# Another bank for the y of the second chunk, and a fixed order between the copies of the state and the low part

## The chip, the cores and the metric

The kernel runs on one core of a Trainium2 chip. The metric is device time in microseconds (us) of one execution, as a median over several. The profile comes from one more execution, taken by the hardware profiler; its span is the time from its first to its last instruction.

## What is computed

The inputs are `x` (4 x 8 x 768 x 32), a decay `a`, `B` and `C` (4 x 8 x 768 x 16), and two weight matrices. A linear recurrence over the 768 positions of each of 4 sequences and 8 heads is computed in chunks, with a state of 16 x 32 per head that goes from one chunk to the next. Its output, 3072 tokens of 256 numbers, goes through a two-layer network:

```python
for c in range(nc):
    M = einsum('bhin,bhjn->bhij', Cc, Bc) * L          # L: causal decay inside the chunk
    y[:, :, sl] = einsum('bhij,bhjd->bhid', M, xc) + einsum('bhin,bhnd->bhid', Cc, state) * decay_to_i
    state = decay_full * state + sum_j(Bc * xc * decay_from_j)
h = x @ w_in                 # 3072 x 256 times 256 x 2048
return (h - tanh(h)) @ w_out # 2048 x 256
```

The result does not depend on the length of a chunk; the kernel takes its own.

## The kernel before

**The recurrence.** A chunk has 112 positions (`Q = P - N`), the last of a sequence fewer; 7 chunks make a sequence, 28 the whole (`ck` = 0 to 27). A chunk's work is a chain: products of C and B into the tile `att` on TensorE (lines 377 in the first three chunks, 437 and 443 later), exponentials on ScalarE (384, 447), their product on VectorE (389, 451), the causal mask on GpSimd (394, 454) which leaves `lt`, and then `chunk_y` (472 to 529). `chunk_y` does the following.

- Line 488: TensorE makes the output y of the chunk from `lt` and `x`. The first 16 rows of `x` of a chunk hold the state that enters it.
- Line 496: TensorE makes the next state from the weighted B (`bw`, made by GpSimd on line 330 for two chunks at a time) and the same `x`, into other columns of the same tile y.
- Line 501: ScalarE copies the state into the first 16 rows of the next chunk's `x`, in four copies.
- Line 508: ScalarE copies y into `xh`, rounded to the format in which TensorE is fast (the high part).
- Line 513: VectorE makes `xl`, y minus the high part (the low part).

The tile y has one buffer, one bank of PSUM (`ps_y`, tag "y"). So line 488 of a chunk waits until lines 501, 508 and 513 of the chunk before are done. ScalarE and VectorE are also kept from reading the one bank at the same time: an instruction of one of them on it waits for the other's instructions that stand before it in the written order. Another single bank, `ps_o` (tag "po"), takes sums of the decays at the start (`pq2`, read by line 786) and from then on the output of the second layer.

**The network.** `mm1(t, u)` (line 547, 12 matmuls of 128 x 256) makes one 256 x 256 piece of h for tile t of 256 tokens from `xh`, `xl` and the split weights `wh`, `wl`; `act` takes tanh on ScalarE (561), h - tanh(h) on VectorE (565), a high part on ScalarE (569) and a low part on VectorE (576); `mm2` (line 597, 12 matmuls) adds it to the output tile `o`. The first tile needs chunks 0, 1 and 2. The first four tiles are taken together in sweeps over pairs of u (u = 0 and 1 first), so that the weights, which `conv` (282 to 306) splits mostly on VectorE, are made as they come.

**The order of the instructions** is made before the kernel runs. Each piece of work is an `op(engine, cost, function, r=, w=, dma=, after=)` of the class `Order` (46 to 188), which records what it must wait for. `schedule` is a list scheduler with the estimated costs, and `issue` takes the best of 16 jittered rounds from a fixed seed (133908) and writes the instructions in the order of their planned starts. The order of each engine is then fixed; in the run, each engine waits for what its next instruction needs. The instructions of `chunk_y` are three to six such ops: TensorE's work of one chunk, four copies of the state, the high part, the low part. The chunks from `JOINT` on have the products of the next chunk in the same TensorE op.

**DMAs** are issued by the SyncE queue (SP). The decays' partial sums go to DRAM and come back in eight transfers for chunks 3 to 9 and eight for the later chunks (`get_parts`, lines 772 and 774); chunk 3's products on line 437 need the first eight.

Of the kernel before, what the change touches and what calls it, by code (L numbers as in the profile page):

```python
# [10 lines left out]
F32 = mybir.dt.float32  # L11
# [9 lines left out]
P = 128  # L21
NB, H, S, D, N = 4, 8, 768, 32, 16
# [10 lines left out]
CPG = 2  # L33
# [14 lines left out]
class Order:  # L48
# [12 lines left out]
    def slot(self, tag, bufs):  # L61
        k = self.count[tag] = self.count.get(tag, -1) + 1
        self.fresh[f"{tag}#{k}"] = tag, f"{tag}#{k - bufs}"
        return f"{tag}#{k}"
# [8 lines left out]
    def __call__(self, eng, cost, fn, r=(), w=(), dma=0, after=()):  # L73
        i = len(self.ops)
        hard = {self.writer[n] for n in r if n in self.writer} | set(after)
        soft, chain = set(), set()
        for n in w:
            hard |= self.readers.pop(n, set())
            if n in self.writer:
                j = self.writer[n]  # L80
                if dma and self.ops[j][0] == "DMA":
                    chain.add(j)
                    hard |= self.before[n]
                else:
                    hard.add(j)
            self.writer[n] = i
            whole = self.whole.get(n, n)
            if whole in self.fresh:
                tag, old = self.fresh.pop(whole)
                for o in (old, *self.parts.get(old, ())):  # L90
                    self.dead.add(o)
                    hard |= self.readers.pop(o, set())
                    if o in self.writer:
                        hard.add(self.writer[o])
                if tag in self.taken:
                    soft.add(self.taken[tag])
                self.taken[tag] = self.made[whole] = i
            elif whole in self.made:
                soft.add(self.made[whole])
        for n in (*r, *w):  # L100
            assert n not in self.dead and n not in self.fresh and n in self.writer, n
        for n in r:
            self.readers.setdefault(n, set()).add(i)
        deps = {j: self.lag(self.ops[j][0], eng) if j in hard else 0.0 for j in (hard | soft) - {i}}
        self.ops.append((eng, cost, fn, deps))
        if dma:

            self.ops.append(("DMA", max(0.25, dma / self.RATE), None, {i: 1.4, **{j: 0.0 for j in chain}}))
            for n in r:
                self.readers[n].add(i + 1)  # L110
            for n in w:
                self.writer[n], self.before[n] = i + 1, hard - {i}
        return i
# [77 lines left out]
def tile_ssm_moe(ctx: ExitStack, tc: tile.TileContext, a, x, bn, bc, wts, out):  # L191
# [7 lines left out]
    ps_o = ctx.enter_context(tc.tile_pool(name="ps_o", bufs=1, space=PSUM))  # L199
    ps_a = ctx.enter_context(tc.tile_pool(name="ps_a", bufs=1, space=PSUM))  # L200
    ps_y = ctx.enter_context(tc.tile_pool(name="ps_y", bufs=1, space=PSUM))

    op = Order()
    slot = op.slot
    grp = {g: {} for g in range(NG)}
    chs = {c: {} for c in range(NCK)}
    raws, gs, po, n_po, obs, misc = {}, {}, {}, {}, {}, {}

    chunks, ends = {}, 0
    for t in range(NT):  # L210
        b, j = divmod(t, S // TT)
# [130 lines left out]
    def qlen(ck):  # L342
        return QL if ck % CPB == CPB - 1 else Q
# [80 lines left out]
    def chunk_a(ck):  # L424

        d, k, q = grp[ck // CPG], chs[ck], qlen(ck)
        n_l = k["n_l"] = [slot("lt", NL)]
        n_a = k["n_a"] = slot("att", 1)  # L430

        def fn_p():
            at_ = ps_a.tile([P, 4, 4 * P], F32, tag="att", name=f"att{ck}")
            at_ = k["a"] = at_[:, :, 0 : 4 * q].rearrange("p i (k q) -> p i k q", k=4)
            for i in range(4):
                r = slice(32 * i, 32 * i + 9)
                nc.tensor.matmul(out=at_[:, i, 0:2, :], lhsT=lt_c[r, ck], rhs=rt_c[r, :, ck, N : N + q],  # L437
                                 start=True, stop=True)
            bb, cc = operands(ck)
            for w in range(2):  # L440
                for i in range(4):
                    r = slice(32 * i, 32 * i + N)
                    nc.tensor.matmul(out=at_[:, i, 2 + w, :], lhsT=bb[r, w], rhs=cc[r, w, 0:q], start=True, stop=True)  # L443

        def fn_e():
            k["l"] = p3.tile([P, H, Q], F32, tag="lt", name=f"lt{ck}", bufs=NL)
            nc.scalar.activation(k["l"][:, :, 0:q].rearrange("p (i w) q -> p i w q", i=4), k["a"][:, :, 0:2, :], AF.Exp)  # L447

        def fn_m():
            lt = k["l"][:, :, 0:q].rearrange("p (i w) q -> p i w q", i=4)  # L450
            nc.vector.tensor_tensor(out=lt, in0=k["a"][:, :, 2:4, :], in1=lt, op=ALU.mult)  # L451

        def fn_s():
            nc.gpsimd.affine_select(out=k["l"][:, :, 0:q], in_=k["l"][:, :, 0:q], pattern=[[0, H], [1, q]],  # L454
                                    compare_op=ALU.is_ge, fill=0.0, base=N, channel_multiplier=-1)

        s = ck >= SPAN[0].stop
        k["rest"] = fn_e, fn_m, fn_s
        k["pe_a"] = fn_p, [d["n_bc"], l_c[s], r_c[s]], [n_a]
        if ck < JOINT:  # L460
            op("PE", 0.65, fn_p, r=k["pe_a"][1], w=k["pe_a"][2])
            chunk_b(ck)
# [9 lines left out]
    def chunk_y(ck):  # L472

        d, k, q = grp[ck // CPG], chs[ck], qlen(ck)
        b, c = divmod(ck, CPB)
        cg = ck % CPG
        n_y = slot("y", 1)
        last = c == CPB - 1
        if c == 0:
            seq[b]["n_xh"] = op.pieces(slot("xh", 2), CPB)  # L480
            seq[b]["n_xl"] = op.pieces(slot("xl", 2), CPB)
        n_xh, n_xl = seq[b]["n_xh"][c], seq[b]["n_xl"][c]

        def fn():
            y = k["y"] = ps_y.tile([P, 2 * H * D], F32, tag="y", name=f"y{ck}")
            for hg in range(2):
                for h in range(4):
                    nc.tensor.matmul(out=y[D * h : D * h + D, hg * Q : hg * Q + q],  # L488
                                     lhsT=d["x"][:, cg, P * hg + D * h : P * hg + D * h + D],
                                     rhs=k["l"][:, 4 * hg + h, 0:q], start=True, stop=True)  # L490
            if not last:

                for w in range(2):
                    for i in range(4):
                        h = 2 * i + w
                        nc.tensor.matmul(out=y[D * i : D * i + N, H * D + D * w : H * D + D * w + D],  # L496
                                         lhsT=d["b"][:, cg, N * h : N * h + N], rhs=d["x"][:, cg, D * h : D * h + D],
                                         start=True, stop=True)

        def fn_c(i):  # L500
            nc.scalar.copy(grp[(ck + 1) // CPG]["x"][0:N, (ck + 1) % CPG, 2 * D * i : 2 * D * i + 2 * D],  # L501
                           k["y"][D * i : D * i + N, H * D : H * D + 2 * D])

        def fn_h():
            if c == 0:
                seq[b]["xh"] = p3.tile([P, 2, S], F32R, tag="xh", name=f"xh{b}", bufs=2)
            k["yv"] = k["y"][:, 0 : 2 * Q].rearrange("p (g q) -> p g q", g=2)[:, :, 0:q]
            nc.scalar.copy(seq[b]["xh"][:, :, c * Q : c * Q + q], k["yv"])

        def fn_l():  # L510
            if c == 0:
                seq[b]["xl"] = p3.tile([P, 2, S], F32R, tag="xl", name=f"xl{b}", bufs=2)
            nc.vector.tensor_tensor(out=seq[b]["xl"][:, :, c * Q : c * Q + q], in0=k["yv"],  # L513
                                    in1=seq[b]["xh"][:, :, c * Q : c * Q + q].bitcast(F32), op=ALU.subtract)

        r, w, cost = [*k["n_l"], d["p_x"][cg], d["n_bw"]], [n_y], 0.5 if last else 0.7
        if JOINT <= ck + 1 < NCK:

            chunk_a(ck + 1)
            fn_p, r_a, w_a = chs[ck + 1]["pe_a"]  # L520
            op("PE", cost + 0.45, lambda: (fn(), fn_p()), r=r + r_a, w=w + w_a)
            chunk_b(ck + 1)
        else:
            op("PE", cost, fn, r=r, w=w)
        if not last:
            for i in range(4):
                op("ACT", 0.2, lambda i=i: fn_c(i), r=[n_y], w=[grp[(ck + 1) // CPG]["p_x"][(ck + 1) % CPG]])
        op("ACT", 0.36, fn_h, r=[n_y], w=[n_xh])
        op("DVE", 0.4, fn_l, r=[n_y, n_xh], w=[n_xl])


    def mm1(t, u):
# [116 lines left out]
    after = cp.tile([P, P], F32, name="after")  # L649
# [119 lines left out]
    def get_parts(i, k, sl):  # L769
# [17 lines left out]
       r=[n_pq2], w=["wdec"])  # L787
# [95 lines left out]
```

## Time and profile before

| | |
|---|---|
| Median of 3 runs | 349.26 us (344.88 to 349.93) |
| The profiled execution | 344.03 us, span 342.3 us |
| TensorE busy | 328.4 us, 96% of the span |
| VectorE busy | 227.5 us, 66% |
| ScalarE busy | 192.8 us, 56% |
| GpSimd busy | 52.1 us, 15% |
| Granted TensorE clock, mean | 0.979 |

How to read it: PE is TensorE, PEld its weight loads, DVE VectorE, ACT ScalarE, POOL GpSimd, SP SyncE. The table of windows gives the busy time of each engine in a stretch of the span, with the number of instructions, then the granted TensorE clock (PEclk, 1.00 is full speed), the busy share of the DMA engines and what they moved. A row of the timeline gives start and duration in us, engine, line, operation, tiles and how many instructions were merged in it (neighbours overlap, since instructions are pipelined); in square brackets is the idle time of the engine just before it, with the instruction that is taken to have ended it. A row of the waits gives total time, number and longest.

### The profile page before, as it was taken

The numbers are of one execution on the slowest core, as the hardware profiler recorded it, in microseconds if no ns is written. First come the engines' busy times: TensorE is split into PE (matmuls) and PEld (weight loads), VectorE is DVE, ScalarE is ACT, GpSimd is POOL, SyncE is SP. The second block draws the span as 40 slices with busy tenths as digits, with TensorE's granted clock in tenths as the row PEclk, the third lists the DMA queues.
The fourth block names the chain that finished last, engine by engine and source line by source line (L and its number), as shares of the span: only waits on it lengthen the run. The fifth ranks groups of instructions, "written<-read, shape, count | busy, mean of one in ns | idle before, by whom it ended". The sixth has DMA issues, their size and how long they took to land.

```text
span 342.3 us, 8855 instructions
## 1 busy us (share of the span) xinstructions
PE 328.4 (96%) x3756; PEld 317.9 (93%) x3756; DVE 227.5 (66%) x339; ACT 192.8 (56%) x403; POOL 52.1 (15%) x69
## 2 busy tenths in 40 slices
PE   8669879999999999999999999999999999999995
PEld 7658769999999999999999999999999999999995
DVE  5998999988889656744755644644655654644552
ACT  8866698767453445634745644634645654634441
POOL 1535443101000001210211210210211110100000
PEclk9956999999999999999999999999999999999999
DMA  5939595800000022300301210210100000100000
GB/s 173 280 92 288 138 314 129 250 23 21 11 2 0 2 64 77 104 1 2 97 9 31 65 29 2 63 29 2 63 3 3 31 2 2 33 0 2 33 0 32
DMA packets 12471, 21.39 MB, mean 62 GB/s; under 512 B 2848, under 2 KB 7648, under 8 KB 12432
## 3 DMA queue, kind: packets, MB, share of 16 engines
q1 hardware_dynamic: 12432, 20.84, 20.9%
q8 instruction: 29, 0.48, 0.6%
q14 instruction: 10, 0.08, 0.1%
HBM read 17.51 MB, written 3.32 MB: 61 GB/s over the span
## 4 chain that ended last, share of the span: by engine, by line
PE 88%; DMA 3%; DVE 3%; SPq 2%; ACT 1%; issue 1%; POOL 1%; POOLq 0%
PE ph L547 40%; PE o L597 40%; PE y L488 4%; PE att L443 3%; DMA raw<-w_d 2%; DMA bc<-bc_d 1%; PE att L437 1%; SPq L232 1%; PE y L496 1%; DVE lt L451 1%; DVE wm L295 0%; DVE gl L576 0%; DVE wv L299 0%; POOL bw L330 0%; ACT x L501 0%
## 5 line engine op out<-in xcount | busy, mean ns | idle before, releaser
L561 ACT ACTIVATE g<-ph 128x512 f32<-128x512 f32 x96 | 57.4, 598 | 82.5 <-PE ph L547 78.7
L565 DVE TENSOR_TENSOR g<-ph,g 128x512 f32<-128x512 f32 x96 | 66.1, 689 | 55.0 <-ACT g L561 54.1
L547 PE MATMUL ph<-xh,wh 128*128 128x256 f32 x384 | 101.5, 287 | 0.0
L547 PE MATMUL ph<-xh,wl 128*128 128x256 f32 x384 | 100.3, 282 | 0.0
L576 DVE TENSOR_TENSOR gl<-g,gh 128x512 fp32r<-128x512 f32 x96 | 68.4, 713 | 28.7 <-ACT gh L569 27.4
L569 ACT CAST gh<-g 128x512 fp32r<-128x512 f32 x96 | 59.3, 619 | 34.1 <-DVE g L565 32.9
L547 PE MATMUL ph<-xl,wh 128*128 128x256 f32 x384 | 77.1, 282 | 0.0
L547 PEld LDWEIGHTS ph<-xh,wh 128*128 128x128 f32 x384 | 73.2, 191 | 1.4 <-issue 0.4
L547 PEld LDWEIGHTS ph<-xh,wl 128*128 128x128 f32 x384 | 73.2, 191 | 0.0
L597 PE MATMUL o<-gh,wh 128*128 128x256 f32 x384 | 62.3, 284 | 0.0
L597 PE MATMUL o<-gh,wl 128*128 128x256 f32 x384 | 60.7, 280 | 0.0
L597 PE MATMUL o<-gl,wh 128*128 128x256 f32 x384 | 60.7, 280 | 0.0
L547 PEld LDWEIGHTS ph<-xl,wh 128*128 128x128 f32 x384 | 59.6, 191 | 0.0
L597 PEld LDWEIGHTS o<-gh,wh 128*128 128x128 f32 x384 | 51.9, 188 | 1.5
L597 PEld LDWEIGHTS o<-gl,wh 128*128 128x128 f32 x384 | 52.0, 188 | 0.0
L454 POOL TENSOR_SCALAR_AFFINE_SELECT lt<-lt 128x896 f32<-128x896 f32 (+1 forms) x25 | 28.3, 1131 | 155.4 <-DVE lt L451 152.8
L597 PEld LDWEIGHTS o<-gh,wl 128*128 128x128 f32 x384 | 51.9, 188 | 0.0
L451 DVE TENSOR_TENSOR lt<-att,lt 128x896 f32<-128x896 f32 (+1 forms) x25 | 26.7, 1067 | 11.0 <-ACT lt L447 10.9
L447 ACT ACTIVATE lt<-att 128x896 f32<-128x896 f32 (+1 forms) x25 | 22.6, 905 | 11.0 <-PE att L443 10.6
L501 ACT COPY x<-y 16x64 f32<-16x64 f32 x96 | 19.4, 202 | 7.9 <-DVE xl L513 6.9
L488 PE MATMUL y<-lt,x 128*32 128x112 f32 (+1 forms) x448 | 17.1, 272 | 6.5 <-POOL bc L337 2.5
L330 POOL TENSOR_TENSOR bw<-braw,wdec 128x256 f32<-128x256 f32 x14 | 12.5, 896 | 52.8 <-PE y L496 47.1
(70 smaller groups left out, 227.2 us busy)
## 6 DMA issues: line engine op xcount, KB each, us to landing
raw<-w_d SPq DMA_DIRECT2D x16, 512.0 KB
x<-x_d SPq DMA_DIRECT2D x14, 256.0 KB
bc<-bc_d SPq DMA_DIRECT2D x56, 60.0 KB
out_d<-ob SPq DMA_DIRECT2D x24, 128.0 KB
braw<-bn_d SPq DMA_DIRECT2D x14, 112.0 KB
cum<-parts SPq DMA_DIRECT2D x1, 168.0 KB
lt_c<-cum SPq DMA_DIRECT2D x4, 27.0 KB
rt_c<-cum SPq DMA_DIRECT2D x4, 27.0 KB
```

What stands on the lines that cost most here:

```text
L330: nc.gpsimd.tensor_tensor(out=d["b"].rearrange("p c (h n) -> p c h n", h=H), in0=d["braw"].rearrange("p c (h n) -> p c h n", h=H), in1=wd. ...
L447: nc.scalar.activation(k["l"][:, :, 0:q].rearrange("p (i w) q -> p i w q", i=4), k["a"][:, :, 0:2, :], AF.Exp)
L451: nc.vector.tensor_tensor(out=lt, in0=k["a"][:, :, 2:4, :], in1=lt, op=ALU.mult)
L454: nc.gpsimd.affine_select(out=k["l"][:, :, 0:q], in_=k["l"][:, :, 0:q], pattern=[[0, H], [1, q]], compare_op=ALU.is_ge, fill=0.0, base=N, ...
L488: nc.tensor.matmul(out=y[D * h : D * h + D, hg * Q : hg * Q + q], lhsT=d["x"][:, cg, P * hg + D * h : P * hg + D * h + D], rhs=k["l"][:, 4 ...
L501: nc.scalar.copy(grp[(ck + 1) // CPG]["x"][0:N, (ck + 1) % CPG, 2 * D * i : 2 * D * i + 2 * D], k["y"][D * i : D * i + N, H * D : H * D + ...
L547: nc.tensor.matmul(out=ph[:, j, :], lhsT=w_[:, u, 0, k, j * P : (j + 1) * P], rhs=d[("xh", "xl")[p]][:, k, ts], start=p == 0 and k == 0 an ...
L561: nc.scalar.activation(g, gs[t, u][0], AF.Tanh)
L565: nc.vector.tensor_tensor(out=g, in0=ph, in1=g, op=ALU.subtract)
L569: nc.scalar.copy(gh, gs[t, u][1])
L576: on.tensor_tensor(out=gl, in0=g, in1=gh.bitcast(F32), op=ALU.subtract)
L597: nc.tensor.matmul(out=po[t, seg][:, e, :], lhsT=w_[:, u, 1, j, e * P : (e + 1) * P], rhs=g[:, j, :], start=u == seg[0] and k == 0 and j = ...
```

## The change

Three things are changed.

- The y of chunk 1 is made in the bank of the output (`ps_o`, tag "po") instead of `ps_y`. All other chunks keep `ps_y`.
- After line 508, which now stands first, the order of the copies of the state and the low part is fixed. For chunks 0 and 1 the low part comes after the four copies. For all later chunks that have a next state, the four copies come after the low part. Before, the planner chose.
- In `Order`, a transfer into a tile into which an earlier transfer goes gets a soft edge from the op that issued the earlier one (`j - 1`), so the planner issues them in the order in which they are written. It adds no wait.

```diff
@@ class Order, __call__ @@
                 if dma and self.ops[j][0] == "DMA":
                     chain.add(j)
+                    soft.add(j - 1)
                     hard |= self.before[n]
@@ chunk_y @@
-        n_y = slot("y", 1)
+
+        n_y = slot("po" if ck == 1 else "y", 1)
...
-            y = k["y"] = ps_y.tile([P, 2 * H * D], F32, tag="y", name=f"y{ck}")
+            y = k["y"] = (ps_o if ck == 1 else ps_y).tile([P, 2 * H * D], F32, tag="po" if ck == 1 else "y", name=f"y{ck}")
...
-        if not last:
-            for i in range(4):
-                op("ACT", 0.2, lambda i=i: fn_c(i), r=[n_y], w=[grp[(ck + 1) // CPG]["p_x"][(ck + 1) % CPG]])
+
         op("ACT", 0.36, fn_h, r=[n_y], w=[n_xh])
-        op("DVE", 0.4, fn_l, r=[n_y, n_xh], w=[n_xl])
+        i_l = [] if ck < 2 else [op("DVE", 0.4, fn_l, r=[n_y, n_xh], w=[n_xl])]
+        i_c = [] if last else [op("ACT", 0.2, lambda i=i: fn_c(i), r=[n_y], after=i_l,
+                                  w=[grp[(ck + 1) // CPG]["p_x"][(ck + 1) % CPG]]) for i in range(4)]
+        if ck < 2:
+            op("DVE", 0.4, fn_l, r=[n_y, n_xh], w=[n_xl], after=i_c)
```

Since the planner works on the whole program, its order can come out otherwise in other places too.

## The prediction

> **What bounds the kernel now.** I read the page's slices first (TensorE's row), then the table of windows for the early part.
>
> ```profile
> PE   8669879999999999999999999999999999999995
> ```
> ```profile
> 16.00:24.00 8.00, 3.82 (x85) 3.40 (x86) 7.76 (x13) 4.63 (x17) 3.25 (x4) 0.59 0.27 75
> 24.00:32.00 8.00, 7.48 (x84) 6.83 (x88) 6.71 (x9) 4.70 (x8) 4.07 (x4) 0.55 0.90 261
> 32.00:48.00 16.00, 12.72 (x250) 11.56 (x247) 15.77 (x20) 13.26 (x33) 7.24 (x9) 1.00 0.75 229
> ```
>
> A slice is 342.3 / 40 = 8.56 us. From the seventh on, some 50 us into the span, TensorE has no gap until the last, so a microsecond won ahead of that is won at the end. What can be won lies between 16 and 48 us: TensorE (the first column after the length) idles 4.18 + 0.52 + 3.28 = 7.98 us there, and at first it runs at little over half clock (0.59 and 0.55). But VectorE (third column) idles only 0.24 + 1.29 + 0.23 = 1.76 us in the same 32: it splits weights and serves the chunks and the first layer out of the same time. So there are two limits, and VectorE's is the nearer.
>
> Next the timeline at the place of the change: ScalarE, VectorE, TensorE and GpSimd.
>
> ```profile
> 15.35 0.20 ACT L501 COPY x<-y 16x64 f32<-16x64 f32 x1
> 15.58 1.09 ACT L384 ACTIVATE lt<-cp,ncum 128x112 f32<-128x112 f32 x4
> 17.19 0.42 ACT L501 COPY x<-y 16x64 f32<-16x64 f32 x2 [0.52 <-DVE xl L513]
> ...
> 16.77 0.38 DVE L513 TENSOR_TENSOR xl<-y,xh 128x224 fp32r<-128x224 f32 x1
> 17.07 1.15 DVE L389 TENSOR_TENSOR lt<-att,lt 128x448 f32<-128x448 f32 x2
> 20.89 0.38 DVE L513 TENSOR_TENSOR xl<-y,xh 128x224 fp32r<-128x224 f32 x1
> ...
> 17.71 0.97 PE L488 MATMUL y<-lt,x 128*32 128x112 f32 x16 [2.08 <-DVE lt L389]
> 21.37 0.97 PE L488 MATMUL y<-lt,x 128*32 128x112 f32 x16 [2.48 <-POOL bc L337]
> 22.09 0.47 PE L496 MATMUL y<-x,bw 128*16 128x32 f32 x16
> 22.49 0.49 PE L437 MATMUL att<-rt_c,lt_c 9*128 9x224 bf16 x4
> 23.77 0.58 PE L547 MATMUL ph<-xh,wh 128*128 128x256 f32 x1
> ...
> 14.88 0.97 POOL L394 TENSOR_SCALAR_AFFINE_SELECT lt<-lt 128x448 f32<-128x448 f32 x1 [0.16 <-DVE lt L389]
> 17.82 1.56 POOL L394 TENSOR_SCALAR_AFFINE_SELECT lt<-lt 128x448 f32<-128x448 f32 x2 [1.97 <-DVE lt L389]
> 19.35 1.07 POOL L330 TENSOR_TENSOR bw<-braw,wdec 128x256 f32<-128x256 f32 x1
> ```
>
> The y of chunk 1 starts at 17.71. Its mask was done at 14.88 + 0.97 = 15.85. What came last were two copies of chunk 0's state, 17.19 to 17.61, held behind the low part of 16.77, which itself stood in VectorE's queue. The releaser in the bracket had no part in it: that product feeds chunk 2. The y of chunk 2 starts at 21.37, just behind chunk 1's low part, which ends at 20.89 + 0.38 = 21.27 and sets the one bank free; the GpSimd copy in the bracket is only a near event. Chunk 2's mask (19.38) and weighted B (20.42) were there earlier.
>
> **The change part by part.** *Copies ahead of the low part, chunk 0.* Four copies behind the high part would end near 15.35 + 4 x 0.21 = 16.19 and let chunk 1's y start at 16.3 instead of 17.71: a gain of 1.4 us. If the exponentials (15.58, 1.09 us) keep their place, the copies end near 17.1 and the gain is 0.6; if the order stayed as it is, 0. I take 1.4, since a list scheduler sends what is ready. The two copies that go ahead delay the exponentials by 0.42 us, to 16.67 + 0.42 = 17.1, but the second of VectorE's two products, which takes the last of them, starts only at about 17.6: covered, else 0.42. The low part keeps its 0.38 us, only later.
>
> *Chunk 1 in the other bank.* The instructions and shapes stay. Two waits go: chunk 1's y for the low part of chunk 0, and chunk 2's y for that of chunk 1. The waits that come are with the bank's tenants:
>
> ```profile
> 10.04 0.41 ACT L786 ACTIVATE wdec<-pq 128x224 f32<-128x224 f32 x1
> ...
> 32.51 0.74 PE L597 MATMUL o<-gh,wh 128*128 128x256 f32 x4
> ```
>
> The tenant before is read out at 10.45; the one after starts at 32.51, 11.2 us behind the low part (21.27). So this costs nothing, and would only if that low part came 11 us later. Chunk 2's y can then start at 19.38 and its state at 20.42, ending near 20.42 + 0.47 = 20.9 instead of 22.56: 1.7 us earlier at best, 0 at worst.
>
> *What is late next.* Behind it in TensorE's queue stand chunk 3's products (22.49) and then the first `mm1` (23.77). The products need eight transfers; the last is issued here:
>
> ```profile
> 20.47 0.70 SPq L772 DMA_DIRECT2D lt_c<-cum  x1
> ```
>
> It landed between 21.17 and 22.49. So the products, and `mm1` with them if it keeps its place, gain between 0 and 1.3 us; if `mm1` goes ahead of them, up to 1.7. The soft edge on the issues permutes transfers of one size into one tile: I take 0, with one issue, 0.70 us, as bound to either side.
>
> And VectorE needs the time. Its idle time behind the first `mm1` is in two waits:
>
> ```profile
> 29.52 1.09 DVE L451 TENSOR_TENSOR lt<-att,lt 128x896 f32<-128x896 f32 x1 [0.54 <-ACT lt L447]
> ...
> 31.95 0.69 DVE L565 TENSOR_TENSOR g<-ph,g 128x512 f32<-128x512 f32 x1 [0.74 <-ACT g L561]
> ```
>
> An earlier `mm1` shortens both: a gain of 0 to 1.28 us at the end. I take 0.9, nearer to the upper end, since what is won at chunk 2 (1.7) is more than either of them.
>
> *Low part ahead of the copies, chunks 2 and later.* Nothing is added, but the copies now wait for a VectorE that is full. Behind them in ScalarE's queue stand exponentials, tanh and splits of weights, and TensorE's next y waits for the copies. Chunk 3 has the opposite order:
>
> ```profile
> 34.10 0.64 ACT L501 COPY x<-y 16x64 f32<-16x64 f32 x3
> 34.83 0.38 DVE L513 TENSOR_TENSOR xl<-y,xh 128x224 fp32r<-128x224 f32 x1
> 35.70 0.59 PE L488 MATMUL y<-lt,x 128*32 128x112 f32 x16
> ```
> ```profile
> ACT x L501 <- DVE xl L513: 6.9, 13, 1.5
> DVE xl L513 <- ACT x L501: 4.2, 10, 0.6
> ```
>
> With the low part first (to 35.21), four copies end at 35.21 + 0.85 = 36.06, and the next y starts 0.36 us later than its 35.70. Where copies stood behind a low part, ScalarE waited up to 1.5 us for it; where they were mixed, the low part waited up to 0.6 for a copy, which a single order may save. Four chunks, 3 to 6, have their next y ahead of 48 us: between -0.6 and 4 x 1.5 = 6.0 us. I take 0.3, near the 0.36 of the one place where the turn can be read off.
>
> Sum: -0.9 + 0.3 = -0.6 us, from the profiled execution's 344.03 to 343.4. That execution lies 5.2 us below the median of the three runs and 0.9 below the lowest. Taken off the median, the forecast is 349.26 - 0.6 = 348.7 us, no change that can be told: 2% is 7.0 us.
>
> **The rivals.** *The early stage gains in full.* If `mm1` goes ahead of chunk 3's products, the 1.7 us reach it, and TensorE is busy earlier and with fewer holes, so its clock may come back sooner.
>
> ```profile
> 17.00:18.00 1.00, 0.29 (x8) 0.32 (x12) 1.00 (x3) 0.80 (x3) 0.18 (x1) 0.74 0.07 27
> ...
> 31.00:32.00 1.00, 1.00 (x42) 0.75 (x45) 0.26 (x2) 0.68 (x2) 1.00 (x1) 0.93 1.03 216
> ```
> ```profile
> 28.45 2.85 PE ph L547 x12
> 46.85 1.60 PE ph L547 x12
> ```
>
> The granted clock (0.74 and 0.93, between 1 and a half) places the switches at 17.48 and 31.14. The second `mm1`, from 28.45 in the chain, took 2.85 us at half clock against 1.60 at full. If the clock came back before it, 1.25 more are won: 1.7 + 1.25 = 2.95, to 341.1, or 346.3 off the median. For it: nothing but these waits held chunk 2. Against it: 2.95 is more than VectorE's whole idle time of 1.76, so VectorE would have to put off splits of weights, and chunk 3's products, once behind `mm1`, delay the later chunks. The Trainium skill, "TensorE: Matmul & The Clock Gate", Part 1, has the gate decide in free-running windows of about 3.4 us, full clock after a window that was busy. The trace agrees: 31.14 - 17.48 = 13.66 us is four of them. By that rule the next earlier return is near 27.7, ahead of the second `mm1`, and the 1.25 us come whole or not at all. The same part of the Trainium skill says that the phase of the windows varies from run to run, which speaks against counting on them.
>
> *Hidden anyway.* Chunk 3's products wait for the transfer until 22.4, `mm1` stays behind them, VectorE's two waits stay: 0, 349.3. For it: the landing is known only to lie before 22.49, and VectorE is full. Against it: the 1.28 us of waits are there to be filled.
>
> *The copies behind the low part set the pace: slower.* In chunks 3 to 6 the copies wait for the low part in VectorE's full queue, and TensorE's next y with them. It decides from the point where the copies end after the next chunk's mask. Halfway to the longest wait, 4 x 0.75 = 3.0 us, less the 0.9 won before: +2.1, 351.4. For it: VectorE's 15.77 of 16 us. Against it: the planner knows the edge and can put the low part first, and chunk 3's 0.36 is small.
>
> *Another order elsewhere.* The planner is a jittered search over the whole program; one changed edge can move instructions anywhere. After 50 us TensorE has no gap, so there this can only lose: two missed `mm1` of 1.41 us are 2.8, 352.1 us. Nothing in the profile speaks for a place.
>
> **How the numbers follow.** Forecast 0.42, full gain 0.20, hidden 0.13, slower by the copies 0.17, another order 0.08. The range goes from the full gain in the profiled execution's own terms, 341, to the slow rivals' 352; it also spans the 5 us by which the executions of before differ. Over 2% faster needs nearly all of the 7.98 us, or the full gain and such a difference between executions: 0.07. Over 2% slower needs the upper bound of 6.0 and more, or the like: 0.07. Within: 0.86.
>
> **What would show it.** Right: chunk 1's y starts near 16.3, chunk 2's between 19.4 and 20.5, `mm1` between 22 and 23.7, VectorE idles under 0.7 us between 24 and 32, and TensorE's last gap ends about 0.6 us earlier. Wrong: a clock that is back before 28 us (full gain); products of chunk 3 still at 22.5 with the same waits behind them (hidden); waits of ScalarE's copies for the low part far over 6.9 us with gaps of TensorE before y between 32 and 48 us (slower); gaps of TensorE after 50 us (another order).

## The result, and the profile after

The changed kernel is a little slower. Over 22 runs of each, its median is 349.37 us (347.90 to 351.74) and that of the kernel before 345.40 us (343.58 to 349.93); the ratio is 1.0124, with a 95% interval of 1.0104 to 1.0145. That is under the 2% that count as a difference here, but it is 4.3 us (0.0124 x 345.4) and its interval excludes no change. The median of the first three runs of before (349.26) lies near the upper end of the 22; its profiled execution (344.03 us, span 342.3) was the more typical one. Medians are of all executions of a kernel; ratios leave out those that took over 1.5% longer than its fastest. The changed kernel's profiled execution took 349.77 us, with a span of 348.0.

What the 5.7 us between the two spans consist of is read from TensorE, which has work until the end. It was busy 328.4 us before and is 331.4 now: 3.0 us more for the same 3756 matmuls, mostly a matter of the clock: in its windows below TensorE is busy 5.6 us at half clock (2.19 + 3.41) where the kernel before had full clock, which is some 2.8 us of lost work. The other 2.7 us are idle time. First the page's slices of the changed kernel, TensorE's busy time and its granted clock.

```profile
PE   8849869999999999999999999999999999999995
PEclk9956969999999999999999999999999999999998
```

The windows of the kernel before behind 48 us, and those of the changed kernel from 16 us on (length, then busy time of TensorE, its weight loads, VectorE, ScalarE and GpSimd, the clock, the DMA share, GB/s):

```profile
48.00:64.00 16.00, 16.00 (x215) 15.29 (x215) 15.66 (x22) 13.95 (x29) 4.15 (x5) 1.00 0.76 192
64.00:120.00 56.00, 56.00 (x518) 55.71 (x517) 48.24 (x68) 30.05 (x52) 3.33 (x5) 1.00 0.09 28
```
```profile
16.00:24.00 8.00, 3.75 (x84) 2.93 (x84) 6.66 (x11) 4.47 (x14) 3.18 (x5) 0.65 0.38 90
24.00:32.00 8.00, 7.37 (x61) 6.42 (x60) 6.85 (x10) 4.25 (x9) 1.22 (x2) 0.50 0.79 226
32.00:48.00 16.00, 11.66 (x232) 10.42 (x224) 15.96 (x20) 12.93 (x28) 7.86 (x8) 0.93 0.75 210
48.00:64.00 16.00, 15.39 (x231) 14.05 (x228) 14.51 (x20) 12.39 (x29) 4.12 (x7) 0.86 0.91 243
64.00:120.00 56.00, 56.00 (x557) 55.41 (x556) 48.23 (x68) 34.47 (x60) 6.73 (x7) 1.00 0.12 36
```

Between 32 and 48 us TensorE now idles 4.34 us where it had 3.28, and between 48 and 64, where it had no gap at all, 0.61. The clock there is 0.93 and 0.86 instead of 1.00. So most of the loss arises between 32 and 64 us, behind the place of the change: the lost clock and 1.67 of the 2.7 us of idle time. From 64 us to its last matmul TensorE is full in both.

The place of the change itself came out nearly as planned. The changed kernel's timeline at TensorE, with the products of chunks 3, 4, 7, 8, 9 and 10 (line 438), VectorE's product of chunk 7, and the last issue of the eight transfers that chunk 3's products need:

```profile
16.50 0.75 PE L490 MATMUL y<-lt,x 128*32 128x112 f32 x16
20.03 0.97 PE L490 MATMUL y<-lt,x 128*32 128x112 f32 x16 [2.66 <-DVE xl L515]
22.80 0.58 PE L551 MATMUL ph<-xh,wh 128*128 128x256 f32 x1 [1.59 <-ACT xh L510]
26.67 0.37 PE L438 MATMUL att<-rt_c,lt_c 9*128 9x224 bf16 x4
31.03 0.37 PE L438 MATMUL att<-rt_c,lt_c 9*128 9x224 bf16 x4
43.41 0.28 PE L438 MATMUL att<-rt_c,lt_c 9*128 9x224 bf16 x4
46.86 0.38 PE L438 MATMUL att<-rt_c,lt_c 9*128 9x224 bf16 x4 [2.73 <-DVE lt L452]
54.28 0.27 PE L438 MATMUL att<-rt_c,lt_c 9*128 9x224 bf16 x4
60.06 0.28 PE L438 MATMUL att<-rt_c,lt_c 9*128 9x224 bf16 x4
...
45.73 1.07 DVE L452 TENSOR_TENSOR lt<-att,lt 128x896 f32<-128x896 f32 x1
...
23.44 0.75 SPq L778 DMA_DIRECT2D rt_c<-cum  x2
```

The kernel before had these products on line 437:

```profile
27.21 0.37 PE L437 MATMUL att<-rt_c,lt_c 9*128 9x224 bf16 x4 [0.52 <-DVE lt L451]
...
43.59 0.28 PE L437 MATMUL att<-rt_c,lt_c 9*128 9x224 bf16 x4
...
48.39 0.27 PE L437 MATMUL att<-rt_c,lt_c 9*128 9x224 bf16 x4
...
54.95 0.28 PE L437 MATMUL att<-rt_c,lt_c 9*128 9x224 bf16 x4
```

The y of chunks 1 and 2 start 1.21 and 1.34 us earlier and the first `mm1` 0.97 us earlier. But in the planner's new order the first `mm1` (22.80) stands ahead of chunk 3's products, which run at 26.67 instead of 22.49. Two things go with that, and no run tells which of them moved the planner: chunk 2 is earlier, and the transfers that chunk 3's products need are issued 3.0 us later (the last issue ends at 23.44 + 0.75 = 24.19 instead of 20.47 + 0.70 = 21.17), so these products could not have run right behind chunk 2 in any case. From there the chunks are late: chunk 4 by 3.8 us (31.03 for 27.21), chunk 10 by 5.1 (60.06 for 54.95). All chunks go through one `att` buffer: products, exponential, VectorE's product, then the next chunk's products. Chunk 8's products stand right behind chunk 7's (43.41) with nothing between; they wait 2.73 us until VectorE has done its product at 45.73 + 1.07 = 46.80. In the waits this is the longest of three, of the changed kernel first, then of the one before (total, number, longest):

```profile
ACT x L503 <- DVE xl L515: 6.2, 8, 1.9
PE att L438 <- DVE lt L452: 3.8, 3, 2.7
```
```profile
PE att L437 <- DVE lt L451: 1.9, 3, 0.8
```

That hole is followed by half clock. The changed kernel's windows of one gate period each (3.41 us, a quarter of the 13.66 us of the prediction):

```profile
38.80:42.22 3.42, 3.13 (x41) 3.03 (x41) 3.38 (x5) 2.73 (x7) 2.19 (x2) 1.00 0.37 90
42.22:45.64 3.42, 1.91 (x58) 1.55 (x57) 3.42 (x6) 3.31 (x6) 2.43 (x2) 1.00 0.40 89
45.64:49.05 3.41, 2.19 (x37) 1.71 (x37) 3.41 (x4) 2.29 (x8) 1.37 (x1) 0.50 0.99 330
49.05:52.46 3.41, 3.41 (x32) 3.17 (x36) 2.74 (x5) 0.91 (x3) 1.14 (x1) 0.50 1.07 371
```

### The profile page after: what moved, and what is told of

Same layout as the page of the kernel before. It is cut to its first block, busy times and chain, and to the rows that moved or that the text cites. A ratio compares the mean times of both kernels' runs of the same rounds, so it can differ in the third digit from the quotient of the medians.

```text
span 348.0 us, 8873 instructions
## 1 busy us (share of the span) xinstructions
PE 331.4 (95%) x3756; PEld 319.4 (92%) x3756; DVE 227.8 (65%) x339; ACT 195.0 (56%) x403; POOL 50.4 (14%) x69
## 4 chain that ended last, share of the span: by engine, by line
PE 84%; DVE 6%; DMA 4%; issue 2%; SPq 1%; POOL 1%; ACT 1%; POOLq 0%; ACTq 0%
PE o L601 38%; PE ph L551 38%; DMA raw<-w_d 4%; PE y L490 3%; PE att L444 3%; DVE lt L452 1%; DVE wm L296 1%; PE att L438 1%; DVE wv L293 1%; DVE g L569 1%; PE y L498 1%; DVE wv L300 1%; DVE wm L288 0%; SPq L233 0%; DVE gl L580 0%
## 5 line engine op out<-in xcount | busy, mean ns | idle before, releaser
L601 PE MATMUL o<-gh,wh 128*128 128x256 f32 x384 | 63.6, 287 | 0.0
L455 POOL TENSOR_SCALAR_AFFINE_SELECT lt<-lt 128x896 f32<-128x896 f32 (+1 forms) x25 | 29.4, 1178 | 164.4 <-DVE lt L452 164.4
L331 POOL TENSOR_TENSOR bw<-braw,wdec 128x256 f32<-128x256 f32 x14 | 11.2, 797 | 57.2 <-PE y L498 54.5
```

The lines of the kernel that those rows point to most:

```text
L331: nc.gpsimd.tensor_tensor(out=d["b"].rearrange("p c (h n) -> p c h n", h=H), in0=d["braw"].rearrange("p c (h n) -> p c h n", h=H), in1=wd. ...
L601: nc.tensor.matmul(out=po[t, seg][:, e, :], lhsT=w_[:, u, 1, j, e * P : (e + 1) * P], rhs=g[:, j, :], start=u == seg[0] and k == 0 and j = ...
```

## The experiments

**Theory**: the change's own parts cost and bring nothing that can be measured; the time comes from another written order, which the planner's search made of the changed edges. **Rivals**: the low part ahead of the copies holds up the chunks; the wait of the one `att` buffer and the half clock behind it are the loss; the planner's own estimate of its plan tells the time. The diffs below show the lines that matter, some of them shortened with `...`, and the remarks behind `#` explain them.

### The parts in the old order

These kernels keep the order of before on TensorE and VectorE and move nothing but the copies and, in the third, the issues of transfers. The first has chunk 1's y in the output's bank and, for chunk 0, copies 3 and 4 right behind copy 2.

```diff
+                if order.index(low) < max(order.index(i) for i in copies):   # ck < 2
+                    order[at:at] = rest        # copies 3 and 4, right behind copy 2
-            y = k["y"] = ps_y.tile(...)
+            y = k["y"] = (ps_o if ck == 1 else ps_y).tile(...)
```

> The order of the kernel before is kept instruction by instruction; only two things change: y of chunk 1 is made in the bank of the output, and the third and fourth copy of chunk 0's state stand behind the second, ahead of the exponentials. Theory A (the planner's new order of the whole program makes the loss, not the edits where they stand) and theory B (the copies behind the low part in the later chunks make it) both expect the predicted gain here: 0.3 to 1.0 us under before. A third, C (the first tile's edits lose by themselves, for instance through the bank or a delayed exponential), expects 1 us or more over before. In the profile: y of chunk 1 near 16.5, of chunk 2 near 19.5 us.

Measured: 345.29 us, ratio 1.0005 (0.998 to 1.0029). Its timeline at TensorE:

```profile
16.02 0.81 PE L499 MATMUL y<-lt,x 128*32 128x112 f32 x14
...
18.92 1.58 PE L499 MATMUL y<-lt,x 128*32 128x112 f32 x16 [1.88 <-POOL lt L405]
...
22.68 0.58 PE L559 MATMUL ph<-xh,wh 128*128 128x256 f32 x1
...
27.81 0.38 PE L448 MATMUL att<-rt_c,lt_c 9*128 9x224 bf16 x4 [1.78 <-DVE lt L462]
```
The first `mm1` is 1.09 us earlier than before (23.77), as hoped. Then chunk 4's products wait 1.78 us for VectorE and start at 27.81, 0.6 us later than before. The whole gain is gone 5 us later: VectorE was the limit. None of the three theories had expected that; two wanted a gain of 0.3 to 1.0 us, the third a loss of 1 us.

The second has only the low part ahead of the copies, for chunks 2 and later.

```diff
+            if ck >= 2 and copies:
+                early = [i for i in copies if order.index(i) < order.index(low)]
+                order[at:at] = early           # behind the low part
```

> The order of before is kept on every engine but ScalarE, where in chunks 2 and later those copies of the state that stood ahead of the low part are moved right behind it. Nothing else of the change. Theory A: within 0.5 us of before, since the waits themselves are short and only a few copies move. Theory B: 3 us or more over before, with gaps of TensorE ahead of y between 32 and 48 us.

Measured: 345.19 us, ratio 0.9994 (0.9963 to 1.0024). The turn costs nothing that can be told. The next has all parts of the change in the old order of TensorE, VectorE and GpSimd.

```diff
+                    soft.add(j - 1)
+                    order[at:at] = rest        # ck < 2
+                order[at:at] = early           # ck >= 2
+            y = k["y"] = (ps_o if ck == 1 else ps_y).tile(...)
```

> All three parts of the change (bank, copies ahead of the low part in chunk 0, low part ahead of the copies from chunk 2 on, the soft edge on DMA issues), but on TensorE, VectorE and GpSimd every instruction stays where it stood before; only ScalarE's copies and the issues of DMAs into one tile change places. Theory A (the planner's new order makes the loss): within 0.5 us of before. Theory B' (the parts hurt together, though not alone): 2 us or more over before.

Measured: 346.14 us, ratio 1.0015 (0.9985 to 1.0044). All that the change says, without the new plan, costs 0.5 us, and by the interval 1.5 at most. Nor is it quite nothing: its twelve executions, granted 0.978 to 0.983, average 346.2 us, and the 15 of before beside them at 0.979 to 0.984 average 344.7. The change as planned loses 4.3 us, so most of the loss is the new order.

### The plan of other edges and other seeds

First the change without the fixed turn for the later chunks, planned anew; then before with only that turn, planned anew.

```diff
-        i_c = [] if last else [op("ACT", 0.2, ..., after=i_l, ...) for i in range(4)]
+        i_c = [] if last else [op("ACT", 0.2, ..., after=[], ...) for i in range(4)]
```

> The changed kernel without the fixed order in chunks 2 and later; the planner chooses anew. Theory A: a new draw, whose own planned span is 1.6 us longer than that of before (the changed kernel's is 2.7 longer), so about 1.6 us over before. Theory B: the loss is gone and the gain of the first tile is left, 0.5 us under before or better.

Measured: 348.94 us, ratio 1.0096 (1.0064 to 1.0128).

```diff
-        op("DVE", 0.4, fn_l, r=[n_y, n_xh], w=[n_xl])      # in the kernel before
+        i_l = [op("DVE", 0.4, fn_l, r=[n_y, n_xh], w=[n_xl])]
+        op("ACT", 0.2, lambda i=i: fn_c(i), r=[n_y], after=i_l, ...)      # ck >= 2
```

> The kernel before with the fixed order (low part, then the copies) in chunks 2 and later alone; the planner chooses anew. Its own planned span is 3.0 us longer than that of before. Theory A: about 3 us over before. Theory B: the whole loss of the change and the missing gain of the first tile, 4 us or more over before. A fourth, D (the loss sits in the DMA order, with the second weights fetched later), expects no loss here if the order of the weights' transfers stays as in before.

Measured: 352.44 us, ratio 1.0202 (1.0169 to 1.0236). The planned spans were 1.6 and 3.0 us over that of before, and the times are 3.3 and 7.0 us over. The same turn that costs nothing in the old order costs 2% when the plan is made anew around it. The three runs that follow change only the seed of the search: before twice, the change once.

```diff
-    SEED = 133908
+    SEED = 1118      # before;  70: the change;  1: before, again
```

> The kernel before with the planner's seed 1118 in place of 133908, nothing else; its planned span is 338.55 us against 334.99, among the worst of 1200 seeds. Theory A: slower by at least the 3.6 us of the plan, some 349 to 353 us, with holes of TensorE ahead of 64 us and a longer stretch at half clock. Theory B': no change, since nothing of the change is in it.

> The changed kernel with the planner's seed 70, nothing else; its planned span is 334.94 us, as that of before (334.99; the changed kernel's own is 337.68). Theory A: back to before, 344 to 346.5 us. Theory B': still 348 us or more.

> The kernel before with seed 1, whose planned span of 336.32 us is the median of 1200 seeds. Theory A: 1.3 us of plan and, at the rate of the two planned runs before (3.3 of time for 1.6 of plan, 7.0 for 3.0), some 2 to 3 us over before: 347 to 348. Theory B': no change.

Measured: 349.69 us, ratio 1.0083 (1.0041 to 1.0126); 350.48 us, 1.0134 (1.0094 to 1.0174); 346.50 us, 1.0012 (0.9986 to 1.0039). A seed alone moves the kernel before by 0.1 to 0.8%. And the planner's own estimate is no safe guide to which plan is good: the change has 337.68 us in it and with seed 70 334.94, as good as the 334.99 of before; on the chip seed 70 was no better than the change. That every new plan is a mere draw is not shown: the two plans with before's edges lost 0.1 and 0.8%, the four with changed edges (the change, its seed 70 and the two above) 1.0 to 2.0%, so the edges may also steer the planner to worse orders. Six plans do not separate the two.

### The hole and the clock

These add matmuls on constants, whose output is not used, where TensorE would wait: ahead of chunk 8's products in the changed kernel (6); there and ahead of y of chunks 1 and 2 (2 and 8); ahead of y of chunks 1 and 2 in the kernel before (7 and 8); and there with 6 more ahead of y of chunk 7.

```diff
+    FILL = {("a", 8): 6}       # then {("y", 1): 2, ("y", 2): 8, ("a", 8): 6}
+    FILL = {("y", 1): 7, ("y", 2): 8}      # before; then with ("y", 7): 6
+            for i in range(FILL[key]):
+                nc.tensor.matmul(out=pw[0:32, i % 4, :], lhsT=one[:, 0:32], rhs=one, start=True, stop=True)
```

> The changed kernel, with 6 matmuls on constants (128x32 by 128x128, their result is read by nobody) put into TensorE's queue ahead of chunk 8's products, where TensorE stands idle for 2.7 us at 44 us; nothing else moves. Theory G (the hole costs twice: by itself, and by the half clock that follows it from 45.6 to 52.5 us): the clock stays at 1.00 through that stage and the time falls by 2 to 3 us, to 346.5 to 347.5. Theory H (VectorE sets the pace there, so TensorE's clock doesn't matter): within 0.7 us of the changed kernel's 349.4.

> As e9, with such matmuls also ahead of the y of chunk 1 (2) and of chunk 2 (8), in the holes at 16 and 17.4 us. Theory G: the clock is not taken away at 18.3 us, or comes back earlier than 32 us; another 1 to 3 us, 344 to 346. Theory H: as e9, since VectorE is full from 22 us on.

> The kernel before, with 7 such matmuls ahead of the y of chunk 1 and 8 ahead of that of chunk 2, in the two holes of TensorE at 15.6 and 18.9 us. Theory G: full clock through to the first layer, the two first pieces of which take 1.4 us instead of 2.85, so 1 to 3 us under before. Theory H: within 0.7 us of before.

> As e11, with 6 matmuls ahead of the y of chunk 7 as well, in the hole at 44.3 us, which in the profiled execution of before did not cost the clock but may in others. Theory G: under e11 by up to 1 us, and a narrower spread of the executions than the 6 us of before. Theory H: within 0.7 us of before, with the same spread.

Measured: 348.31 us, ratio 1.0087 (1.0052 to 1.0121); 348.15 us, 1.0097 (1.0061 to 1.0133); 345.93 us, 1.003 (1.0002 to 1.0059); 344.12 us, 0.9965 (0.9938 to 0.9991). The profiled execution of the first took 800.67 us and is not read. The second, the changed kernel filled at all three places:

```profile
16.00:24.00 8.00, 4.43 (x101) 3.97 (x102) 5.96 (x11) 4.65 (x15) 3.35 (x5) 0.99 0.41 99
24.00:32.00 8.00, 7.37 (x44) 6.20 (x44) 7.61 (x10) 3.38 (x7) 1.06 (x2) 0.50 0.65 185
32.00:48.00 16.00, 13.20 (x236) 11.99 (x236) 14.40 (x18) 12.83 (x26) 7.44 (x8) 0.94 0.68 196
48.00:64.00 16.00, 13.69 (x244) 12.28 (x243) 15.97 (x21) 13.05 (x30) 6.03 (x6) 1.00 0.96 276
```

The mean clock is 0.984, above the 0.979 of before, and the kernel is still 1% slower. TensorE now idles 2.31 us between 48 and 64 us: what the clock gives, it waits for. Filling wins 0.3 points of the ratio (1.0124 to 1.0097), some 0.9 of 4.3 us, and the two intervals overlap: the clock is a small part of the loss. Theory G, which wanted 346.5 to 347.5 us and then 344 to 346, fails in both; theory H fits better, though the first is 1.1 us under the change where it allowed 0.7. In the kernel before the early filling cost 0.3% instead of winning 1 to 3 us. The last of the four beats both kernels by a little, 0.35% below before. With both kernels filled throughout (clocks 0.983 to 0.989 and 0.988 to 0.998), the change is still 4.0 us slower (348.15 less 344.12).

### Which part of the order

Lists in which the order of before and that of the change are joined at a time of the plan: pieces planned up to 24 or 48 us come in the one order, the rest in the other. All have chunk 1's y in the output's bank.

```diff
-        for i in sorted(range(n), key=lambda i: (start[i], i)):
+        for i in ORDER:
```

> All that the plan of before starts in its first 24 us stands in the order that the changed kernel gives it, everything else in the order of before; y of chunk 1 in the bank of the output. Theory E (the loss is made early, by the later transfer of the second weights): about 349. Theory L (it is made behind 24 us): within 1 us of before, 344.5 to 346.5.

> The other way round: the first 24 us in the order of before, everything else in that of the changed kernel; y of chunk 1 in the bank of the output. Theory E: within 1 us of before. Theory L: about 349.

> The first 48 us of the plan in the new order, the rest in that of before. Theories E and L, in so far as L means the stretch from 24 to 48 us: about 349. Theory M (the loss is made behind 48 us, by the order of the sweeps): within 1 us of before.

> The first 48 us in the order of before, the rest in the new one. Theories E and L: within 1 us of before. Theory M: about 349.

| order up to 24 us | 24 to 48 | from 48 | median, us | ratio |
|---|---|---|---|---|
| new | old | old | 345.98 | 1.0030 (1.0003 to 1.0057) |
| old | new | new | 349.45 | 1.0154 (1.0115 to 1.0192) |
| new | new | old | 349.97 | 1.0163 (1.0130 to 1.0196) |
| old | old | new | 346.86 | 1.0064 (1.0028 to 1.0101) |

Where the new order holds between 24 and 48 us, 1.5% is lost; where it does not, 0.3 to 0.6%. So the stretch from 24 to 48 makes most of the loss, the early order by itself 1 us, and the late order by itself 2.2 (0.0064 x 344.6); with the new order between 24 and 48 neither adds anything, so these parts do not sum.

Two of these runs also speak on the first `mm1`. Their chunk 3's products, of "new, old, old" first, then of "old, new, new", with the latter's first `mm1` and chunk 4's products:

```profile
24.95 0.72 PE L478 MATMUL att<-rt_c,lt_c 9*128 9x224 bf16 x2 [1.64 <-DMA rt_c<-cum]
```
```profile
21.90 0.39 PE L478 MATMUL att<-rt_c,lt_c 9*128 9x224 bf16 x4
...
23.07 0.58 PE L588 MATMUL ph<-xh,wh 128*128 128x256 f32 x1
...
30.68 0.37 PE L478 MATMUL att<-rt_c,lt_c 9*128 9x224 bf16 x4
```

In "new, old, old" the late transfers hold part of chunk 3's products until 24.95, and the kernel loses only 0.3%. In "old, new, new" they run at 21.90, ahead of the first `mm1` (23.07), and it loses 1.5% all the same: chunk 4's products are at 30.68. So the first `mm1` ahead of chunk 3's products is not what costs the time.

In that stretch the chunks are set back, by pieces of the first layer that stand ahead of them on ScalarE, VectorE and TensorE. The last two runs test that: the kernel before with chunks 3 and 4 set back and nothing else, and the mixed order "old, new, new" with the two set forward again. The edits are lists of numbers; in words, the first moves the following.

```diff
@@ the kernel before: TensorE @@
 mm1(0, 0)
-products of chunk 4
 mm1(0, 1)
+products of chunk 4
@@ ScalarE @@
-exponential of chunk 3
 tanh(0, 0)
+exponential of chunk 3
-exponential of chunk 4
 tanh(0, 1)
+exponential of chunk 4
@@ VectorE @@
-product of chunk 3
 split of the second weights (wl)
+product of chunk 3
```

> The kernel before (no part of the change in it) in its own order, but with the chain of chunks 3 and 4 set behind pieces of the first layer: chunk 3's exponential behind the first tile's first tanh, its product on VectorE behind the second split, chunk 4's products behind the first tile's second mm1, and its exponential and product behind that one's tanh. Theory N (the change loses because first-layer pieces stand ahead of chunks 3 and 4, so that every later chunk, which passes through one att buffer, comes later): 347.5 us or more where the kernel before has 345.4, a ratio over 1.006, and chunk 10's products at 57 us or later instead of 54.95. Rival (the loss lies in another place of the order between 24 and 48 us): within 1 us of the kernel before.

> The run with before's order up to 24 us and the change's behind it (349.45 us), with the inverse moves: chunk 3's exponential right behind the first mm1, its product ahead of the second unit's split and of the first tanh, chunk 4's products ahead of the second mm1, and its exponential and product ahead of that one's tanh. Theory N: 346 to 347 us, a ratio of 1.002 to 1.006, and chunk 10's products earlier than the 60 us they had, at 58 us or before. Rival: 348.5 us or more, since the later part of the order keeps the loss.

Measured: 348.12 us, ratio 1.0085 (1.0052 to 1.0118), and 347.71 us, 1.0069 (1.0042 to 1.0096). The products of chunks 4 and 10 of the first, then those of chunks 4, 5, 8 and 10 of the second with the matmuls of the second layer ahead of chunk 5's:

```profile
30.95 0.37 PE L478 MATMUL att<-rt_c,lt_c 9*128 9x224 bf16 x4
...
59.22 0.28 PE L478 MATMUL att<-rt_c,lt_c 9*128 9x224 bf16 x4
```
```profile
27.05 0.38 PE L478 MATMUL att<-rt_c,lt_c 9*128 9x224 bf16 x4 [1.24 <-DVE lt L492]
...
33.96 0.74 PE L638 MATMUL o<-gl,wh 128*128 128x256 f32 x4 [0.76 <-DVE gl L617]
34.63 0.28 PE L478 MATMUL att<-rt_c,lt_c 9*128 9x224 bf16 x4
...
45.96 0.37 PE L478 MATMUL att<-rt_c,lt_c 9*128 9x224 bf16 x4 [2.73 <-DVE lt L492]
...
59.46 0.28 PE L478 MATMUL att<-rt_c,lt_c 9*128 9x224 bf16 x4
```

The first came out as the theory wanted: chunk 10 is 4.3 us later than before and the kernel 0.85% slower. The second is between the two expectations and bears out neither: the ratio falls from 1.0154 to 1.0069, and chunk 10 comes 2.4 us earlier than the 61.83 of the mixed order, but not at 58. Chunk 4 is back at 27.05; chunk 5, at 34.63, still stands behind the second layer (in the kernel before its products run at 31.85, ahead of that layer's 32.51), and the wait of 2.73 us ahead of chunk 8 is still there.

A comparison at equal clock makes these two weaker. Executions of before beside them that were granted 0.979 to 0.983 took 343.9 to 345.6 us, those at 0.974 346.6 to 347.3. The first run had only one at 0.980 (347.05) and four at 0.975, 347.0 to 348.1. The mixed order's one execution at 0.980 took 347.79, and the second run at 0.979 to 0.980 took 346.8 to 348.2. So a good part of what the two moves cost and win goes with the clock. The change itself had four executions at 0.977 to 0.980, and they took 347.9 to 348.7, some 3.6 us (348.3 less 344.7, the means) over before at that clock: there the order costs its time without the clock.

## Why the prediction was right and wrong

**Right: the place of the change.** The y of chunk 1 was to start near 16.3 and starts at 16.50; that of chunk 2 between 19.4 and 20.5, at 20.03; `mm1` between 22 and 23.7, at 22.80. The bank had no other tenant in the way, and the copies went ahead. One wait was overlooked: chunk 2's y takes the one bank from chunk 0 now, whose low part the change puts later (19.39 to 19.78 us), and the bracket at 20.03 names it. So the start at 19.38, the best case, was not to be had.

**Wrong size: -0.9 for VectorE's two waits.** It is nothing: 1.0005 in the run with the old order. VectorE's idle time between 24 and 32 us was to fall under 0.7 and is 8.00 - 6.85 = 1.15 with the change (1.29 before). The sum had VectorE as the nearer limit and yet credited it with 0.9; in that run chunk 4's products waited 1.78 us for VectorE instead.

**Wrong size: +0.3 for the low part ahead of the copies.** 0.9994: nothing either. ScalarE's wait for it even fell in the changed kernel, from 6.9 to 6.2 us. The rival that had this edit set the pace fell with it.

**The step that failed: the sum took the rest of the order as it stood.** Its terms were read off the old timeline, and the new plan was put at nothing. With all three parts in the old order the ratio is 1.0015: 0.5 us over before, at most 1.5, where the sum said 0.6 under. With the plan made anew it is 1.0124, 4.3 us, so some 3 to 4 of them are outside the sum, and most come from the order between 24 and 48 us. The rival "another order elsewhere" was what happened. It had a chance of 0.08, and its place was mostly wrong: it looked behind 50 us, where the changed kernel has one gap of 0.61 us. "Nothing in the profile speaks for a place", it said. Something did: the rival "full gain" named the danger, chunk 3's products behind `mm1` and the later chunks late. It was kept as a reason against a gain and never priced as a loss. The runs show the danger one step on: wherever the new order holds between 24 and 48 us, chunk 4's products are late (30.68 to 31.03 instead of 27.21), whether chunk 3's are early or late.

**A bound that did not hold: the transfers.** The soft edge on the issues was put at 0, with 0.70 us either way. In the new plan the last issue ends 3.0 us later. With the soft edge in the old order it ends at 21.22, against 21.17, so this too is the new plan and not the edge. By the run "new, old, old" it is part of a loss of 0.3%.

**Wrong base.** The predicted 348.7 lies near the measured 349.37 only because two errors cancel: it was taken off a median of three that was 3.9 us over the later median of 22, and the change went the other way.

**The clock.** The stage of half clock did not end earlier:

```profile
18.00:19.00 1.00, 0.00 (x0) 0.00 (x0) 1.00 (x3) 0.66 (x3) 0.59 (x1) 0.67 0.56 90
31.00:32.00 1.00, 1.00 (x21) 0.96 (x20) 0.23 (x1) 0.86 (x2) 0.13 (x1) 0.51 1.04 384
```

By the clocks of these two it runs from 18.34 to 31.98 us, 13.64, four periods of 3.41, as before; the second stage (45.64 to 52.46) has two. That agrees with the windows that the Trainium skill, "TensorE: Matmul & The Clock Gate", Part 1, describes. The same part of the Trainium skill has half clock follow an idle window. Here it followed the window from 42.22, in which TensorE was busy for 1.91 of 3.42 us; by this measurement a window that is 56% busy can be enough.

**What stays open.** That the order between 24 and 48 us makes most of the loss is shown. That it works through the late chain of chunks 3 and 4 is shown in part: setting it back costs 0.85%, setting it forward wins back half. How much of either is the clock, and whether chunk 5 behind the second layer makes the rest, was not separated. Why the planner's search came to this order, the earlier chunk 2, the later transfers or chance, was not tested.

Over the two kernels and 16 of the 18 runs (not the filled one with 800.67 us, and not the first other seed of before, whose profiled execution was its longest), the time goes with the start of chunk 10's products, with a correlation of 0.88 and 0.8 us per microsecond; some of them:

| kernel | chunk 10's products, us | median, us |
|---|---|---|
| before | 54.95 | 345.40 |
| low part first, old order | 55.64 | 345.19 |
| before, another seed (1) | 56.47 | 346.50 |
| chunks 3 and 4 set back | 59.22 | 348.12 |
| after | 60.06 | 349.37 |
| old order to 24 us, then new | 61.83 | 349.45 |

This is a correlation and no test. Each start is from one profiled execution, whose clock need not be that of the median, and a stage of half clock delays both.

## What to carry to other kernels

Where a search writes the order of the instructions, any changed edge gives a new order: hold the old order first, to see what the edit is worth, and count the spread over seeds (up to 0.8% here) as a price of the new plan. When a wait goes away, ask which pieces may now change places, on every engine and in the transfers, and price what falls behind; here chunk 4 was 3.8 us late, and chunk 10, behind it in a chain through a single buffer, 5.1. The 1.09 us that were won ahead of the full VectorE were gone 5 us later.

## What was not expected of the hardware

The granted clock of the kernel before falls into groups, about one gate period of half clock apart. Of the 17 executions beside the last two runs, four at 0.974 took 346.58 to 347.27 us (mean 346.9) and eleven at 0.979 to 0.983 took 343.92 to 345.58 (mean 344.7); the two at 0.965 took 346.77 and 349.12. One window of half clock would lose 3.41 / 2 = 1.7 us of work; the two groups differ by 2.2. The kernel before filled with idle matmuls had clocks of 0.988 to 0.998, and its 12 runs lay within 1.7 us of one another (343.39 to 345.08), where 22 of the 23 of before beside it spread over 4.0 (343.43 to 347.38; the other took 349.77): what the filling wins is that the executions at 347 no longer occur among these.

In these windows the way back takes more than the way down. In the kernel before, windows that were 86% and 85% busy at half clock were followed by half clock, the next, which was full, by full clock; and one at full clock that was only 60% busy (2.06 of 3.42) was followed by full clock (1.00 between 48 and 64 us):

```profile
20.89:24.30 3.41, 2.93 (x54) 2.64 (x55) 3.24 (x6) 1.18 (x6) 0.17 (x1) 0.50 0.50 142
24.30:27.72 3.42, 2.90 (x24) 2.71 (x26) 3.42 (x5) 2.32 (x3) 1.06 (x2) 0.50 0.78 238
27.72:31.13 3.41, 3.41 (x28) 3.09 (x24) 2.87 (x4) 1.42 (x2) 2.14 (x3) 0.50 1.04 304
...
44.78:48.20 3.42, 2.06 (x44) 2.04 (x44) 3.41 (x5) 3.34 (x10) 1.58 (x2) 1.00 0.99 371
```

A full window is not always enough: in the changed kernel the one below was full, and the clock stayed at half for one more. The trace does not show why.

```profile
25.16:28.57 3.41, 3.41 (x30) 2.72 (x29) 3.41 (x5) 2.50 (x5) 0.00 (x0) 0.50 0.84 183
28.57:31.98 3.41, 3.41 (x31) 3.19 (x31) 2.26 (x4) 1.22 (x3) 1.22 (x2) 0.50 0.97 336
```
